# A gated-attention and MLP kernel: the table that gives small elementwise instructions to VectorE or GpSimd, and the written order, worked out anew

## The chip, the core and the metric

One Trainium2 chip, one of its cores. The metric is the device time of one execution in microseconds, median of three runs. The engines are called as in the profile: PE (TensorE), DVE (VectorE), ACT (ScalarE), POOL (GpSimd) and SP (SyncE, which issues all DMAs here). Each engine takes its own instructions in the order in which they are written, and waits at one whose inputs are not ready, while those behind it wait too.

## The reference

Two parts follow each other. The first is an attention with a complex, data-dependent decay, computed there as a recurrence over 768 steps (B, H, S, D = 4, 8, 768, 48):

```
mag = sqrt(a_re^2 + a_im^2);  a = a * min(mag, 0.999) / (mag + 1e-6)
for t in range(S):
    S_re, S_im = a_t * (S_re + i S_im)        # complex, row by row
    S_re = S_re + outer(k_t, v_t)
    y_t  = q_t @ S_re
```

The second treats y as 3072 tokens of 384 numbers and runs a small MLP over them: `h = y @ w_in` (384 to 2048), `g = h * clip(h + 3, 0, 6) / 6`, `out = g @ w_out` (2048 to 384).

## The kernel before

The 3072 tokens are cut into 24 chunks of 128 steps, and inside a chunk the recurrence becomes matrix products. Thirteen streams of work, each a Python generator, make the instructions:

- **normal** (letters N and O) brings the decays to their allowed size: squares, a logarithm and exponentials on ACT, and products on DVE or POOL (lines 399 to 424; tile `sq`).
- **chain** (C) multiplies the decays up along the 64 steps of each half of a chunk, three chunks at a time, in short DVE instructions (lines 439 to 483; tiles `pr`, `fx`, `z`), and then makes the small factors `t` and `ww` that carry the state from chunk to chunk (lines 489 to 523).
- **prep** (P, Q) makes the scaled keys and queries of a chunk (lines 553 to 569; tiles `gg`, `u`), which a DMA turns into `kq`.
- **mat** (A) runs a chunk's attention: `pA` on PE, masked on DVE into `am` (line 612), the running state (lines 631, 638, 679), and the result `py`, copied by ACT into `xh` (line 698) with its rounding rest `xl` on DVE (line 700).
- **moe** (M) runs the MLP over groups of chunks: seven groups of 2, 2, 4, 4, 4, 4 and 4 chunks. Each has 16 steps: `ph` on PE (line 750), `r` on ACT (line 757), then a product on DVE: `hs` in groups 0 and 1 (line 771), and `ph`, `gh`, `gl` on DVE, ACT, DVE from group 2 on (lines 761, 764, 767), where the products go to PE split into a high and a low half (lines 728 to 730).
- **weights** (W, D), **part** (I) and **wsplit** (S) turn the 16 blocks of weights into the form that PE uses (lines 340 to 358, 794 and 799, 814 and 817), and **verdict** (V) draws one flag `oki` from all range checks (lines 826 to 845); a fallback outside of this text would run if it were 0.

Nothing is scheduled by a tool at the places that matter here: under `manual_schedule` the string ORDER (lines 36 to 64, 2574 letters) says which stream makes its next step, and that is the order of the instructions on every engine:

```python
for x in ORDER:
    assert next(streams[x]) != "wait"
```

Which of the two engines takes one of some 200 small elementwise instructions is read from a second table, ENG (lines 66 to 80), one letter for each place and V for DVE:

```python
s = ENG.get(kind, "")
return V if i < len(s) and s[i] == "V" else P
```

The thirteen kinds stand for lines 402 (a), 412 (b), 555 (c), 561 (d), 799 (i), 523 (n), 817 (o), 489 (p), 631 (s), and 501 to 511 (t, u, v, w). Those of a to d, i, o and s work on 256 to 1024 columns and, all of them, read two inputs from SBUF; the other kinds work on 3 to 18 columns. The buffers matter in one place: `r`, `ot` and the verdict's `one` share a pool of two (tag `r`).

Of the kernel before, what the change touches and what calls it, by code (L numbers as in the profile page):

```python
# [35 lines left out]
ORDER = (
    "ZZNONOODWOWNOONWINWWZNOZOWNODNONOOWDNNDWQNNNWONINOWNOOWOZNNWONOOCWWCWCCCIZCWCCCCDDWCCNWCCCCWCWCN"
    "WCCWCCWCOCWCCCNCWINOCDCICCCNCNCWCWWWCDCCCCCCCCWCOWIWICOPCCOCCIWWWWCWPQPQPPWQPNWWQOWWOPPCPCNQPNDW"
    "WIWOWQPPPIPPDPWWQOCPAWWNPOQPQWCAWQWQWPWADCCPCACWQPAAWCAAPIAWWZWAWCICCCWWAPCIACCCCWCCWZAAWNWCACWA"
    "AAACPNCCACCCCCCPWADCAWAWWNWWAAACACADCNOCNOMMCMNCMMMWPWCACAWCCICAACAMWNCWMCAMMMCWCMWCMMONMWOMCWMC"  # L40
    "WACAMMMMCMMCWMCNMCMNIWMPMMMOWPMMWADCMCOPWPPMAWPOMMMODPCPCMOMMMWMAPMOWWMIICPCPAMIPPMIICCMMCCMIMCC"
    "APCCMPMCMPMPCMMMMMWPAAMMAMCCAMMPWMAAAMACDCIPWCMWCAPWAMMCAIPMPAMMCAMMWMWAMPWPPCMWPCWMCCWMCPCCAMCI"
    "CCCAWCWAWWCPMWMMCMPICMICMMMAMMAMCMCCCMAAMPMMMMMPCPCAMPCCMPZWCMAMMMMMCWMACWCPMSMAMMMZCAAPSAMMCMSC"
    "AMMMMAPPNMMMNSCASAINPMMPMMSMCMPCSPMOMAMIPNPMASPNNOAAMPMMMOPMPMPPMMAAOMNSONSMAAAAMAAMMMMCOAMOAMAA"
    "MPSCIMANOMOSMMMPSPAONPMMPMAMMPACPCPCMMAMSCPMMAMMMMPPPPMCSPMCACCAMAMMSMCIPACMAAAMMCCSMMMMPMMCAPIC"
    "CPCAMASACMCMMPMMCCPMMMCAMAMCCCMCACSPMAMSAASCCMMMIMAPAMMPMCCMMACZMMCMAACMMMZMCSCACSAAMPAMANMCMCCC"
    "AMCCNCCPAAMMMPMMCMCCMAOCANMNNMMAAACCCMMSCMMSMAMMSMPAAPMMMAOMPMPMAMNPMPNMPPMNMMMMPSCMMOOMPOSMMAOM"
    "NAMMPMMAOCMMCMAAMPMOMCMSNPMOMMPOMPMPCMCPAMMCCMPMPACPMMMCMMAACAMCMCMACACCPMMMMAMCPCMMCMCPPMMMMMCP"
    "CCCCCMMMAMAPPMCCMMMPMMCMMMCAPMAMMSCCMCCAMCMPMMMAPPMCMMAAPCPMCCCMMCCMCCMCMMMACMSPPMACMZAMMMCMNMCM"
    "ACMCCCCMPMANPPMCCPAMAMMNMAMMMMNAPAPAMPPMMMMAMMAMAMZNNAMPPAMMPOMPOAPMMNCPMOAPOMMOMMANMPPOAAAMACPM"  # L50
    "PMMCNMPAMPPSMCMMMOOMAMPAAOMMAMMMNMPMMMAMMPOPMPCPPMCMPACCMMPMMAAMCMPCCCAMCAPCAMCMMCPCMMMAMMACMMCM"
    "AAPCCCMACMCACMMCPPCPMMAAPMZMMAMAMCAMCMMCMMMZMMACCACMMCPCCMCMMNAMCCCNAAOMCMMNMMAACOCCMACNCCPMCMNA"
    "MPMNMCMNMMCMAAMCCMAMMMOMMMCAMAMCCMACONOMMAMMMMOMPAMPPMCAMMAAAMCOPPMCPAMMMPMMPPOMPMOMPMMNMMMMPAMP"
    "MMMMAOCAAMMPMPNPMMACCMCCAMCPMMCMMMMMPCAMMCCCCCMMPCPPMPAMMMAMAMMCMMCPMCCMMAMAMPPPPMCAMMAMMAAMMCCC"
    "APMPMMMCMACAMPPAMCACCMCMMAPACMAAPAMAMAMMCPCCMAMMMMMPCCMCCCPZCAMACMAMAACMMMZMMCCACCMNCMMNCCMMMCMN"
    "NMAPMCMMMOCMMMMCNAMPMMMMAAACOMNPOCAOOOMMACMMAMMCMPAPMMPMAMPMMMAPOMPPPCPMMMMPMPMMAMPOMMNMMMPPMCNM"
    "OMNAMONCMCPMPMAMAMCAMMMMCPMMMAMCMMAPMMMAPMAMCMMCMPMMCCMMCAMCMMCAAMPMMPMAMMMPMAPPMMCMAMCAMCCPCCPC"
    "AMCCMMAACAAAMMPMCMMCPCMCMAMMMAPCMMMMACMPCMACAPCAMAPAPCMMCCCCMCMPAMCMMMAMMMMMPCMAMAMMACMCMMAPACCM"
    "PAAMCAMMACMAMAMMPPAMCCCMMACMMAMMMACMMAMCMMMMAMACMMPMMPMMAMAPAMAAAPPPMPPCAMMMMMPMPAMMPMAAMCMMMMMM"
    "MMMMMMMMMAAMMMMMPMMMPMMMMAMMAACPPMMMAMAMPMMMMPMPMMMMPAPMMPMACAMMAMMPPMMMMMMAMPMPMMMPAPMPMMMPMMMA"  # L60
    "MMMPAMPPMMAMPMMMMMMAMMAMAMMMPAMMMAMAMPAAMMAPAMMMMAPPMMMMVMMMMMMMAMMMAMMMMAMMAAMAMMMAMAAMMMAMMMMM"
    "MAMMMAMAMMMMMMMMMMMMMMMMMMMMMMMMMMMMMMMMMMMMMMMMMMMMMMMMMMMMMMMMMMMMMMMMMMMMMMMMMMMMMMMMMMMMMMMM"
    "MMMMMMMMMMMMMMMMMMMMMMMMMMMMMMMMMMMMMMMMMMMMMMMMMMMMMMMMMMMMMMMMVMMMMMMMMMMMMM"
)
# [921 lines left out]
```

## Time and profile before

| | |
|---|---|
| median of 3 runs | 686.49 us (686.03 to 686.93) |
| the profiled execution | 686.5 us, its span 684.1 us |
| busy over the span: PE, DVE, ACT, POOL | 575.1, 557.1, 337.0, 138.2 us |
| instructions: PE, DVE, ACT, POOL | 4145, 1091, 636, 138 |
| PE's first matmul | at 71.3 us |
| DVE's first product (line 771) of group 1, and (line 761) of group 2 | ends at 170.8 and 250.8 us |
| ACT's first copy of a group's result (line 780), groups 2 to 6 | at 334.6, 428.1, 518.1, 604.8 and 675.1 us |

The 2.4 us between the span and the time lie around the program. In the rows below, a busy time is a union, while a mean is of single records, which overlap a little on DVE: an instruction's record starts some 0.08 us before that of the one ahead of it ends. A row of the views by line names the line, the engine, the operation, what it writes and reads, the shapes and the count; behind the bar stand the busy time in us and the mean in ns; behind the second bar the idle time just before.

### The profile page before, as it was taken

What the parts mean: (1) busy time and instruction counts of PE and PEld (TensorE: products, weight loads), DVE (VectorE), ACT (ScalarE), POOL (GpSimd) and SP (SyncE); (2) the same over time, 40 slices, a digit from 0 to 9 for tenths busy, and PEclk for the clock granted to TensorE, in tenths of its full rate; (3) what the DMA queues carried; (4) which work ended last, traced back from release to release, by engine and by line L of the source; (5) the groups of instructions that cost most, each with busy time, mean ns of one, the idle gap of its engine ahead of it and who ended that gap; (6) DMA issues with size and microseconds to landing.
All of it is one profiled execution on the core that took longest, in us unless ns stands there. A gap on an engine that the chain in (4) does not pass through costs nothing. (4 is left out here: it accounts for less than half of the span.)

```text
span 684.1 us, 11374 instructions
## 1 busy us (share of the span) xinstructions
PE 575.1 (84%) x4145; PEld 472.2 (69%) x4145; DVE 557.1 (81%) x1091; ACT 337.0 (49%) x636; POOL 138.2 (20%) x138
## 2 busy tenths in 40 slices
...
GB/s 337 117 115 84 235 173 161 36 130 110 148 98 97 121 86 76 75 91 121 135 94 163 3 97 97 167 51 97 86 51 105 97 26 74 62 47 0 1 0 52
DMA packets 51008, 66.97 MB, mean 98 GB/s; under 512 B 11905, under 2 KB 38401, under 8 KB 50945
## 3 DMA queue, kind: packets, MB, share of 16 engines
...
q8 instruction: 35, 0.57, 0.4%
...
## 5 line engine op out<-in xcount | busy, mean ns | idle before, releaser
L757 ACT ACTIVATE r<-ph,half 128x512 f32<-128x512 f32 (+1 forms) x112 | 70.0, 625 | 153.7 <-PE ph L750 153.3
L610 PE MATMUL pA<-kq 96*128 96x128 f32 x384 | 53.0, 288 | 71.9 <-DMA kq<-gg 71.3
L728 PE MATMUL po<-gl,wout_h 128*128 128x512 f32 x240 | 100.4, 418 | 6.4 <-DVE gl L767 6.4
L610 PEld LDWEIGHTS pA<-kq 96*128 96x128 f32 x384 | 51.7, 203 | 74.8 <-DMA kq<-gg 71.3
L761 DVE SCALAR_TENSOR_TENSOR ph<-r,ph 128x512 f32<-128x512 f32 x80 | 55.4, 692 | 58.4 <-ACT r L757 57.7
L729 PE MATMUL po<-gh,wout_l 128*128 128x512 f32 x240 | 95.2, 397 | 0.0
L730 PE MATMUL po<-gh,wout_h 128*128 128x512 f32 x240 | 94.9, 396 | 0.0
L764 ACT ACTIVATE gh<-ph 128x512 fp32r<-128x512 f32 x80 | 47.9, 598 | 84.0 <-DVE ph L761 83.9
L750 PE MATMUL ph<-xh,win_l 128*128 128x512 f32 (+1 forms) x288 | 81.6, 392 | 0.0
L750 PE MATMUL ph<-xh,win_h 128*128 128x512 f32 (+1 forms) x288 | 78.0, 379 | 0.0
L750 PE MATMUL ph<-xl,win_h 128*128 128x512 f32 (+1 forms) x288 | 77.3, 377 | 0.2 <-DVE xl L700 0.2
L767 DVE TENSOR_TENSOR gl<-ph,gh 128x512 fp32r<-128x512 f32 x80 | 55.0, 688 | 26.0 <-ACT gh L764 25.7
L439 DVE TENSOR_TENSOR pr<-z 128x288 f32<-128x288 f32 (+2 forms) x176 | 70.9, 433 | 1.4
L732 PE MATMUL po<-hs,wout 128*128 128x256 f32 x192 | 53.7, 409 | 13.2 <-DVE hs L771 13.1
L750 PEld LDWEIGHTS ph<-xh,win_l 128*128 128x128 f32 x288 | 52.7, 193 | 11.3 <-issue 0.6
L750 PEld LDWEIGHTS ph<-xl,win_h 128*128 128x128 f32 x288 | 51.7, 190 | 10.7 <-DVE xl L700 0.7
L728 PEld LDWEIGHTS po<-gl,wout_h 128*128 128x128 f32 x240 | 45.2, 188 | 19.9 <-DVE gl L767 8.9
L750 PEld LDWEIGHTS ph<-xh,win_h 128*128 128x128 f32 x288 | 51.6, 189 | 10.2 <-issue 0.8
L569 DVE TENSOR_TENSOR gg<-u,z 128x384 f32<-128x384 f32 x92 | 52.7, 618 | 0.3
L730 PEld LDWEIGHTS po<-gh,wout_h 128*128 128x128 f32 x240 | 45.1, 188 | 10.8
L729 PEld LDWEIGHTS po<-gh,wout_l 128*128 128x128 f32 x240 | 45.2, 188 | 8.2
L732 PEld LDWEIGHTS po<-hs,wout 128*128 128x128 f32 x192 | 34.9, 198 | 21.6 <-DVE hs L771 17.1
...
## 6 DMA issues: line engine op xcount, KB each, us to landing
kq<-gg SPq DMA_DIRECT2D x138, 128.0 KB, 4.6
...
```

The costliest lines, as they stand in the source:

```text
L439: V.tensor_tensor(pr[:, j], src, fac[:, j : j + 1].to_broadcast([C, *shape]), ALU.mult)
L569: V.tensor_tensor(gg[:, k, :, 1 - i].rearrange("p d (f s) -> p f d s", f=2), u[:, 2 * i : 2 * i + 2], zv[:, k], ALU.mult,)
L610: T.matmul(pA[:, i], kt[:, hf * 4 + i], qt[:, hf * 4 + i], start=True, stop=True)
L728: T.matmul(po[i], wh, gl, start=f == 0, stop=False)
L729: T.matmul(po[i], WOUTL[f][:, cols], gh, start=False, stop=False)
L730: T.matmul(po[i], wh, gh, start=False, stop=f == NFF - 1)
L732: T.matmul(po[i], WOUT[f][:, cols], hs[0], start=f == 0, stop=f == NFF - 1)
L750: T.matmul(ph, w[:, kt * C : (kt + 1) * C], xx[:, kt], start=t == 0 and kt == 0, stop=last)
L757: A.activation(r, ph, AF.Relu, scale=1.0 / 6.0, bias=half)
L761: V.scalar_tensor_tensor(ph, r, 1.0, ph, ALU.min, ALU.mult)
L764: A.activation(gh, ph, AF.Copy)
L767: V.tensor_tensor(gl, ph, gh, ALU.subtract)
```

## The change

Both tables are new, and nothing else is. ENG gives 126 of its 204 places to DVE where it gave 75: by kind, POOL keeps 3 (was 8) of a, 4 (11) of b, 11 (14) of c, 10 (17) of d, 5 (10) of i, 2 (7) of n, 6 (10) of o, 5 (5) of p, 11 (14) of s, and 21 (33) of t to w. ORDER has the same 2574 letters, each as often as before, in another sequence.

```diff
@@ ORDER, 2 of 27 lines @@
-    "ZZNONOODWOWNOONWINWWZNOZOWNODNONOOWDNNDWQNNNWONINOWNOOWOZNNWONOOCWWCWCCCIZCWCCCCDDWCCNWCCCCWCWCN"
-    "WCCWCCWCOCWCCCNCWINOCDCICCCNCNCWCWWWCDCCCCCCCCWCOWIWICOPCCOCCIWWWWCWPQPQPPWQPNWWQOWWOPPCPCNQPNDW"
...
-    "MMMMMMMMMMMMMMMMMMMMMMMMMMMMMMMMMMMMMMMMMMMMMMMMMMMMMMMMMMMMMMMMVMMMMMMMMMMMMM"
+    "ZZNODONZOWONWOOWDDNNNWWOOZDNWONWONZWONNNWOOOIDNOWONNWONZIONNOWONWNWPCCCCDWCCWCCNWCWCCWCNWCWCCCCC"
+    "CCCCWWCOCWWCNCOCCNCWWCWCOCDCCCCCCDWCNCNCCOWOCCWIWCCCQCIWCCWWCWCWPCOQCOOPWPICQWNPQPWIPQNWWQPQPWPP"
...
+    "MMMMMMMMMMMMMMMMMMMMMMMMMMMMMMMMMMMMMMMMMMMMMMMMMMMMMMMMMMMMMMMMMMMMMVMMMMVMMM"
@@ ENG @@
-    a="PVVPVVPVPVVPPVVVPP",
-    b="VVVPVVPPPPPPVPPPPV",
-    c="VPVPVPVVPPPPVPPVPPVVPPPV",
-    d="PPPVPPVPPPVVPPVVPPPPPPVP",
-    i="VPVPPVVPPPPVPVPP",
-    n="PPPPPPPV",
-    o="PPVVVPPPPPVPPPVV",
-    p="VPPPVPPV",
-    s="PPVPVPPVVPPPPPPVPVVVPVPV",
-    t="PPPVVVPPPPVPPPVP",
-    u="VPPPPPPPPPVPPVPV",
-    v="PPPPVVPV",
-    w="PPPVVVPP",
+    a="PVPVVVVVVVVVVVPVVV",
+    b="PVVVVVVVVVVPPVVPVV",
+    c="VVPVVVPVVPVPPPPPVVPVVPVP",
+    d="VVVPVVVPVVPVPVPPVPPPPVVV",
+    i="PVVPVVVVVPPVVVVP",
+    n="VPVVPVVV",
+    o="VPVVPPVVVVVVVPPP",
+    p="VPVPPPPV",
+    s="PPVVVVVVPVPVPPVVVPPPPVVP",
+    t="VVPVPPVPVPVVPVVV",
+    u="VVVVPPPPPVPVVVPV",
+    v="VPPPPVVV",
+    w="VPPPVVVP",
```

Three places show what that does to the engines' rows. The first is the beginning of POOL's own list, from its first instruction on tensors (`sq` of normal) to the time before PE starts. Before:

```order
L402 TENSOR_TENSOR sq<-sq 128x320
L402 TENSOR_TENSOR sq<-sq 128x256
L412 TENSOR_TENSOR sq<-sq,y_177 128x256
L799 TENSOR_TENSOR win_l<-win,win_h 128x384 x2
L555 TENSOR_TENSOR gge<-gge,ue 128x384
L561 TENSOR_TENSOR gg<-gg,u 128x384
L497 MEMSET ww 128x36
L501 TENSOR_TENSOR t<-pps,z 128x6 x2
L561 TENSOR_TENSOR gge<-gge,ue 128x384
L799 TENSOR_TENSOR win_l<-win,win_h 128x384
```

and now:

```order
L402 TENSOR_TENSOR sq<-sq 128x320
L412 TENSOR_TENSOR sq<-sq,y_133 128x320
L402 TENSOR_TENSOR sq<-sq 128x320
L799 TENSOR_TENSOR win_l<-win,win_h 128x384
L497 MEMSET ww 128x36
L555 TENSOR_TENSOR gg<-gg,u 128x384
L799 TENSOR_TENSOR win_l<-win,win_h 128x384
L489 COPY pps<-z 128x6x3
L561 TENSOR_TENSOR gg<-gg,u 128x384
```

The prep of the early chunk (`gge`) has left POOL, and so has one of the three `win_l` shown; one more step on `sq` of 320 columns has come.

The second place is DVE ahead of the first product of group 1 (`hs`, line 771, the last row of each). Before:

```order
L565 SCALAR_TENSOR_TENSOR u<-gg 128x2x192
L439 TENSOR_TENSOR pr<-z 128x144
L569 TENSOR_TENSOR gg<-u,z 128x2x3x64 x2
L441 TENSOR_TENSOR z<-pr 128x18x4
L443 TENSOR_TENSOR z<-pr 128x18x4
L569 TENSOR_TENSOR gg<-u,z 128x2x3x64 x2
L478 TENSOR_TENSOR fx<-z 128x441
L479 TENSOR_TENSOR z<-z 128x9x7x7
L612 TENSOR_TENSOR am<-pA,cst 128x512
L771 SCALAR_TENSOR_TENSOR hs<-r,ph 128x256
```

and now:

```order
L402 TENSOR_TENSOR sq<-sq 128x576
L478 TENSOR_TENSOR fx<-z 128x441
L479 TENSOR_TENSOR z<-z 128x9x7x7
L478 TENSOR_TENSOR fx<-z 128x441
L479 TENSOR_TENSOR z<-z 128x9x7x7
L481 TENSOR_TENSOR z<-z,fx 128x9x7x7
L483 TENSOR_TENSOR z<-z,fx 128x9x7x7
L412 TENSOR_TENSOR sq<-sq,y_1311 128x576
L478 TENSOR_TENSOR fx<-z 128x441
L479 TENSOR_TENSOR z<-z 128x9x7x7
L799 TENSOR_TENSOR win_l<-win,win_h 128x384
L771 SCALAR_TENSOR_TENSOR hs<-r,ph 128x256
```

Instead of a chunk's prep (lines 565 and 569) and a mask (line 612), the step of the chain (lines 478 to 483) stands there, among it instructions that POOL had: `sq` (lines 402, 412) and `win_l` (line 799).

The third place is the end of SP's list, where the last results are written out and the flag is read. Before:

```order
L584 DMA kq<-gg 16x8x256 x6
L592 DMA vt<-in_vL_dram 128x512
L781 DMA out_dram<-ot 128x512 x3
L879 TENSOR_LOAD oki
L879 ISA x2
L781 DMA out_dram<-ot 128x512 x3
L883 COMPARE_AND_BRANCH
```

and now:

```order
L584 DMA kq<-gg 16x8x256 x6
L592 DMA vt<-in_vL_dram 128x512
L781 DMA out_dram<-ot 128x512 x5
L879 TENSOR_LOAD oki
L879 ISA x2
L781 DMA out_dram<-ot 128x512
L883 COMPARE_AND_BRANCH
```

The flag's load stood ahead of the last three writes, and now stands ahead of the last one alone. On DVE and PE the flag's instructions (lines 836 to 845, 842) have moved to behind the last product and the last matmul of group 6.

## Rows read from the trace of the kernel before

**Rows 1.** The view of windows: busy time of each engine in four stretches. Columns: stretch and its length, busy us (and instructions) of PE, PEld, DVE, ACT and POOL, granted clock of PE as a share, share of the DMA engines, GB/s. The stretches end with PE's first matmul, with DVE's first product of group 1, with its first of group 2, and with the middle of the run behind that.

```profile
0.00:71.30 71.30, 0.01 (x1) 0.04 (x1) 58.01 (x121) 53.31 (x102) 15.22 (x25) 1.00 0.52 164
71.30:170.80 99.50, 84.21 (x578) 69.91 (x578) 97.84 (x208) 63.71 (x123) 28.88 (x22) 0.98 0.57 140
170.80:250.80 80.00, 71.77 (x660) 62.57 (x660) 76.49 (x142) 38.53 (x84) 31.90 (x26) 0.94 0.57 118
250.80:520.00 269.20, 264.32 (x1969) 215.53 (x1970) 251.57 (x501) 127.65 (x238) 53.72 (x55) 1.00 0.45 93
```

**Rows 2.** The timeline of DVE and POOL from 26 to 34 us: start, length, engine, line, operation, what it writes and reads, shapes, count.

```profile
26.51 1.63 DVE L439 TENSOR_TENSOR pr<-z 128x288 f32<-128x288 f32 x2
26.55 1.28 POOL L799 TENSOR_TENSOR win_l<-win,win_h 128x384 fp32r<-128x384 f32 x1 [4.28 <-ACT win_h L794]
...
31.14 0.55 DVE L346 SCALAR_TENSOR_TENSOR wout<-ws 128x384 int32<-128x384 int32 x1
31.61 0.82 DVE L439 TENSOR_TENSOR pr<-z 128x288 f32<-128x288 f32 x2
...
33.77 0.75 DVE L402 TENSOR_TENSOR sq<-sq 128x576 f32<-128x576 f32 x1
```

**Rows 3.** The same view at 212 us.

```profile
212.26 2.01 POOL L631 TENSOR_TENSOR state<-state,cw 96x1024 f32<-96x1024 f32 x1
...
212.40 2.99 DVE L443 TENSOR_TENSOR z<-pr 128x144 f32<-128x144 f32 x1
```

**Rows 4.** Groups by line and shape on DVE from the start to 250.8 us.

```profile
L439 DVE TENSOR_TENSOR pr<-z 128x288 f32<-128x288 f32 x56 | 26.2, 504 | 0.4
L569 DVE TENSOR_TENSOR gg<-u,z 128x384 f32<-128x384 f32 x32 | 20.2, 677 | 0.0
L342 DVE SCALAR_TENSOR_TENSOR ws<-ws 128x768 int32<-128x768 int32 x16 | 16.8, 1052 | 3.4 <-ACT ws L340 3.4
...
L479 DVE TENSOR_TENSOR z<-z 128x441 f32<-128x441 f32 x16 | 12.5, 780 | 0.6
L612 DVE TENSOR_TENSOR am<-pA,cst 128x512 f32<-128x512 f32 x17 | 11.4, 680 | 0.6 <-PE pA L610 0.6
L443 DVE TENSOR_TENSOR z<-pr 128x144 f32<-128x144 f32 x28 | 11.1, 396 | 0.0
...
L346 DVE SCALAR_TENSOR_TENSOR wout<-ws 128x384 int32<-128x384 int32 x16 | 10.8, 676 | 0.0
...
L481 DVE TENSOR_TENSOR z<-z,fx 128x441 f32<-128x441 f32 x8 | 6.5, 810 | 0.0
...
L817 DVE TENSOR_TENSOR wout_l<-wout,wout_h 128x384 fp32r<-128x384 f32 x4 | 3.9, 985 | 0.0
...
L424 DVE SCALAR_TENSOR_TENSOR z<-z,sq 128x320 f32<-128x320 f32 x1 | 1.0, 1030 | 0.0
```

**Rows 5.** The same view from 98 to 117 us, a stretch in which POOL does next to nothing.

```profile
L479 DVE TENSOR_TENSOR z<-z 128x441 f32<-128x441 f32 x4 | 2.5, 619 | 0.1
...
L481 DVE TENSOR_TENSOR z<-z,fx 128x441 f32<-128x441 f32 x2 | 1.2, 610 | 0.0
...
L346 DVE SCALAR_TENSOR_TENSOR wout<-ws 128x384 int32<-128x384 int32 x2 | 1.1, 550 | 0.0
L342 DVE SCALAR_TENSOR_TENSOR ws<-ws 128x768 int32<-128x768 int32 x1 | 1.0, 959 | 0.2 <-ACT ws L340 0.2
...
L799 DVE TENSOR_TENSOR win_l<-win,win_h 128x384 fp32r<-128x384 f32 x1 | 0.6, 551 | 0.0
```

**Rows 6.** The same view from 33.1 to 44.3 us, in which POOL does nothing.

```profile
L439 DVE TENSOR_TENSOR pr<-z 128x288 f32<-128x288 f32 x6 | 2.5, 452 | 0.1
...
L443 DVE TENSOR_TENSOR z<-pr 128x144 f32<-128x144 f32 x3 | 0.9, 299 | 0.0
```

**Rows 7.** Groups by line and shape on POOL from the start to 250.8 us.

```profile
L799 POOL TENSOR_TENSOR win_l<-win,win_h 128x384 fp32r<-128x384 f32 x10 | 12.2, 1220 | 26.8 <-ACT win_h L794 22.3 <-issue 4.6
L817 POOL TENSOR_TENSOR wout_l<-wout,wout_h 128x384 fp32r<-128x384 f32 x9 | 11.1, 1237 | 36.4 <-issue 18.1 <-ACT wout_h L814 12.1 <-ACT kk L623 6.3
L561 POOL TENSOR_TENSOR gg<-gg,u 128x384 f32<-128x384 f32 x6 | 10.1, 1680 | 15.2 <-DMA vt<-in_vL_dram 8.0 <-ACT u L559 7.2
L412 POOL TENSOR_TENSOR sq<-sq,y 128x576 f32<-128x576 f32 x4 | 6.7, 1678 | 13.4 <-ACT y L408 13.4
L631 POOL TENSOR_TENSOR state<-state,cw 96x1024 f32<-96x1024 f32 x3 | 6.6, 2204 | 0.0
L555 POOL TENSOR_TENSOR gg<-gg,u 128x384 f32<-128x384 f32 x3 | 5.5, 1850 | 28.4 <-ACT u L553 28.4
L402 POOL TENSOR_TENSOR sq<-sq 128x576 f32<-128x576 f32 x3 | 5.4, 1811 | 16.3 <-ACT sq L399 16.3
```

**Rows 8.** The view of waits from 170.8 to 250.8 us: who waited for whom, us in total, times, longest.

```profile
PE po L732 <- DVE hs L771: 5.8, 3, 2.8
```

**Rows 9.** The timeline of ACT and of SP's queue at the end.

```profile
675.05 1.30 ACT L780 ACTIVATE ot<-po 128x512 f32<-128x512 f32 x2 [1.85 <-PE po L730]
...
675.68 3.50 SPq L781 DMA_DIRECT2D out_dram<-ot  x3
...
678.22 0.60 ACT L780 ACTIVATE ot<-po 128x512 f32<-128x512 f32 x1 [1.87 <-PEq L883]
```

**Rows 10.** From the page, what the DMA engines moved in GB/s, in 40 equal slices of the span.

```profile
GB/s 337 117 115 84 235 173 161 36 130 110 148 98 97 121 86 76 75 91 121 135 94 163 3 97 97 167 51 97 86 51 105 97 26 74 62 47 0 1 0 52
```

More of the change, by code (lines that the diff above doesn't have):

```diff
@@ L36 @@
 ORDER = (
-    "ZZNONOODWOWNOONWINWWZNOZOWNODNONOOWDNNDWQNNNWONINOWNOOWOZNNWONOOCWWCWCCCIZCWCCCCDDWCCNWCCCCWCWCN"
-    "WCCWCCWCOCWCCCNCWINOCDCICCCNCNCWCWWWCDCCCCCCCCWCOWIWICOPCCOCCIWWWWCWPQPQPPWQPNWWQOWWOPPCPCNQPNDW"
-    "WIWOWQPPPIPPDPWWQOCPAWWNPOQPQWCAWQWQWPWADCCPCACWQPAAWCAAPIAWWZWAWCICCCWWAPCIACCCCWCCWZAAWNWCACWA"
-    "AAACPNCCACCCCCCPWADCAWAWWNWWAAACACADCNOCNOMMCMNCMMMWPWCACAWCCICAACAMWNCWMCAMMMCWCMWCMMONMWOMCWMC"
-    "WACAMMMMCMMCWMCNMCMNIWMPMMMOWPMMWADCMCOPWPPMAWPOMMMODPCPCMOMMMWMAPMOWWMIICPCPAMIPPMIICCMMCCMIMCC"
@@ L42 @@
[L42 to L61, printed above, removed]
@@ L62 @@
-    "MAMMMAMAMMMMMMMMMMMMMMMMMMMMMMMMMMMMMMMMMMMMMMMMMMMMMMMMMMMMMMMMMMMMMMMMMMMMMMMMMMMMMMMMMMMMMMMM"
-    "MMMMMMMMMMMMMMMMMMMMMMMMMMMMMMMMMMMMMMMMMMMMMMMMMMMMMMMMMMMMMMMMVMMMMMMMMMMMMM"
+    "ZZNODONZOWONWOOWDDNNNWWOOZDNWONWONZWONNNWOOOIDNOWONNWONZIONNOWONWNWPCCCCDWCCWCCNWCWCCWCNWCWCCCCC"
+    "CCCCWWCOCWWCNCOCCNCWWCWCOCDCCCCCCDWCNCNCCOWOCCWIWCCCQCIWCCWWCWCWPCOQCOOPWPICQWNPQPWIPQNWWQPQPWPP"
+    "NWNOQPOCCPCPWAIWWWPQCCWQCQPCACAWACDQWAACCWCPIAAPWCPWCPAAACPDWWACWPCAWPCICWWAWCWACQACZCAAACCAACWC"
```

23 lines of the change are left out of this document (added).

## The prediction

> **What bounds the kernel now.** I read the windows first, because the page's shares are means over stages with different limits. Until 71.3 us PE has nothing to do. From there to 250.8 us, where DVE makes the first product of group 2, DVE is busy 174.3 of 179.5 us and PE 156.0 [rows 1]: DVE sets the pace. PE's idle time there is mostly a wait for DVE; near group 1, 5.8 us of it hang on `hs` [rows 8]. From 250.8 to 520 us the roles turn: PE is busy 264.3 of 269.2 us and DVE 251.6 [rows 1]; behind that PE goes on without a gap. So the end is about PE's time from group 2 on, which the change does not alter (the order puts the same matmuls behind that point), plus the moment at which group 2 starts. That moment is DVE's, and the question is what the new tables do to DVE's work up to it.
>
> The second view is DVE's groups by line. Not all of DVE's busy time is work. At 26.5 us two L439 take 1.63 us while a `win_l` runs on POOL for 1.28 us [rows 2]; a pair of them takes 0.82 us a few microseconds later, with POOL idle [rows 2]. At 212.4 us an L443 that takes 0.30 us elsewhere [rows 6] lasts 2.99 us beside a POOL instruction of 1024 columns and 2.01 us [rows 3]. DVE instructions with two inputs in SBUF are held, those that read PSUM are not: L612 keeps its 680 ns beside all of POOL's work [rows 4].
>
> **What the held time amounts to, before 250.8 us.** Count times (mean here less mean where POOL is still) [rows 4 to 6]: L439 56 x (504 - 452) = 2.9 us; L569 32 x (677 - 550, the L346 of the same 384 columns) = 4.1; L479 16 x (780 - 619) = 2.6; L443 28 x (396 - 299) = 2.7; L346 into `wout` 16 x (676 - 550) = 2.0; L481 8 x (810 - 610) = 1.6; L817 4 x (985 - 551) = 1.7. That is 17.6 us. Eleven other forms, from L342 with 16 x (1052 - 959) = 1.5 down to the single L424 with about 0.5 [rows 4, 5], add 12.2. Together 29.8 us, an eighth of DVE's 232.3 busy us there. Up to that point POOL has run 43 instructions of 256 to 1024 columns, the 38 of [rows 7] and five single ones; they have 19,456 columns. So one POOL column costs DVE 1.53 ns: 0.59 us for 384 columns, 0.88 for 576, 1.57 for 1024.
>
> **What the same instruction costs on DVE.** From the start of one 384-column instruction to that of the next it is 31.61 - 31.14 = 0.47 us [rows 2]: its record of 0.55 overlaps the next by 0.08. The same 0.08 off gives 0.67 us for 576 columns (0.75 in [rows 2]) and, by the slope between these two, 1.14 us for 1024. Per column it is cheaper to do the work on DVE than to be held by POOL.
>
> **The change, up to group 2.** By the order DVE gets 13 more instructions of 384 columns (13 x 0.47 = 6.1 us), 8 of 576 (5.4), 3 of 1024 (3.4), 8 small ones of some 0.1 us (0.7), one L414 more and a closing pair of chain products less (-0.4): +15.2 us. POOL keeps 15 of the 43, with 5,824 columns. They will hold DVE for 5,824 x 1.53 = 8.9 us instead of 29.8: 20.9 come back. The three of 1024 columns all leave POOL ahead of that point, and the one that [rows 3] shows cost DVE 2.99 - 0.30 = 2.69 us, where its columns give 1.57. If all three cost that, the others' rate is (29.8 - 8.1) / 16,384 = 1.33 ns and the 15 keep 7.7 us: 22.1 come back. The sum is so 15.2 - 20.9 = -5.7 or 15.2 - 22.1 = -6.9 us; I take -6.5. It lies wholly on the path as long as DVE sets it. The bounds: if each of the 15 held DVE for its own whole length (0.9 to 1.9 us, 20 together, by the means of [rows 7]) it would be +5.7; if none held it, -14.6. I stay with the rate, since the 15 are of the same lines and stand among the same DVE work as the 43.
>
> Moved waits come beside it. DVE's idle time is 13.3 us before PE's start, 5.2 us from there to 250.8 [rows 1], so waits that go can give little after the start; new ones could cost. I take 0, between -5 and +5. The loads: the fourth piece of the first decays goes behind two more blocks of weights of 768 KB on SP; at the 337 GB/s of the first slice [rows 10] that is 4.7 us later at most. ACT has a block of weights to convert ahead of that piece in the new order: 0, at most +4.7. ACT and PE do what they did, in another sequence.
>
> **From group 2 to group 5.** The order adds 4.5 us to DVE here and takes 3,072 POOL columns away, 4.7 us at the rate above: 0, or +4.5 if nothing came back. DVE has 17.6 us to spare in this stretch, PE 4.9 [rows 1], so a part of it is covered. I take +0.5.
>
> **The end.** The flag's nine DVE instructions and its matmul now stand behind the last product. DVE is done with them about 2 us later, when PE has just finished; the second `ot` shares a buffer with the verdict's `one`. The last `ot` starts at 678.22 us in any case, since its buffer waits for the write issued at 675.68 [rows 9], and the flag's load on SP, ahead of the last write, should be through by then. +0.1; +1 if not.
>
> Sum: 686.5 (the profiled execution; the median is 686.49) - 6.5 + 0.5 + 0.1 = 680.6 us, with its own range of 675 to 685.
>
> **A rule that speaks against it.** DVE is the engine that has nothing to spare before 250.8 us [rows 1], and the change gives it more. The Trainium skill, Perfetto Trace Analysis, section "Optimizing Scalar/DVE Operations", says that with DVE saturated it may make sense to offload work, even to GpSimd; it adds that between these two it might not help, because they share a read port. By its first half the move back costs the 15.2 us and the time would be some 702 us; by its second half, which [rows 2, 3] bear out, the held time comes back.
>
> **Rivals.**
>
> 1. *Group 1 does not get shorter (slower).* The gain isn't spread evenly. Up to group 1's first product the order puts 15.5 us more on DVE and takes 6,784 POOL columns (10.4 us) away: that product comes 5.1 us later, at 175.9 us, as more of the chain and of the weights now stands ahead of it. The forecast needs the stretch from there to group 2 to shrink from 80.0 to 68.4 us. If it takes as long as before, group 2 starts 5.1 us late: 686.5 + 5.1 + 0.6 = 692.2 us. It decides from 74.3 us on. For it: PE is busy 71.8 of the 80 us [rows 1], and its list is fixed. Against it: DVE is busy 76.5 there, POOL 31.9 [rows 1], so the held time is largest there, and PE's idle time is a wait for DVE [rows 8].
> 2. *PE sets that stretch.* If PE needs its 71.8 busy us [rows 1] and no less, group 2 starts at 247.7: -3.1, and the time is 686.5 - 3.1 + 0.6 = 684.0 us.
> 3. *The held time does not come back (slower).* The 15 that stay would have to hold DVE 2.0 us each for that, 29.8 in all as before; then the 15.2 us come on top: 686.5 + 15.2 = 701.7 us. Against it: those lines last 1.2 to 1.9 us as a mean (all but L631, which is gone there) [rows 7].
> 4. *More than forecast.* The waits that shrink, too: a third of the 13.3 us before PE's start and PE's 4.9 us later [rows 1], -9: 671 to 675.
> 5. *Nothing to be seen.* New waits on DVE of about 6 us eat the gain: 685 to 688.
>
> **How the numbers follow.** Forecast 0.53; rivals 1 to 5: 0.17, 0.11, 0.03, 0.10, 0.06. A measurement of this kernel can tell about 0.2% from no change, that is 685.1 to 687.9. Faster: 0.53 + 0.10 + half of rival 2 (0.06) = 0.69. Within 0.2%: the other half and rival 5 = 0.11. Slower: rivals 1 and 3 = 0.20. The predicted time is the forecast's. The range reaches down to 671 for rival 4 and up to 690, which takes in rivals 2 and 5 and the nearer half of rival 1; I leave out its farther half, rival 3 and a little below, some 0.15.
>
> **What would show it.** In the new profile POOL's instructions should fall to some 85 and its busy time to about 80 us, DVE's busy time should stay within 10 us of 557 although it has 51 more instructions, and the means of L439, L569 and L443 up to group 2 should drop to within 30 ns of 452, 550 and 299. Group 1's first product should come near 176 us, group 2's first near 244, and each later group's results 5 to 8 us earlier than 334.6, 428.1, 518.1, 604.8 and 675.1. PE's first matmul should come about a microsecond before 71.3. The prediction is wrong in its main step if those means stay up, in its second if the stretch of group 1 stays near 80 us with DVE idle, and in its third if the gain at group 2 is there and is lost later.

## The result, and the profile after

| | before | after |
|---|---|---|
| median of the runs | 686.26 us (684.15 to 686.93, 4 runs) | 665.98 us (664.57 to 669.69, 4 runs) |
| the profiled execution, its span | 686.5, 684.1 us | 666.9, 665.0 us |
| DVE's first product of group 1 ends | 170.8 | 168.1 (forecast 175.9) |
| DVE's first product of group 2 ends | 250.8 | 233.1 (forecast near 244) |
| from there to the first product of group 5 | 273.1 us | 272.2 us (forecast +0.5) |
| from there to the end | 160.2 us | 159.7 us |

The ratio is 0.9718, with an interval of 0.9671 to 0.9764: faster, and by 20 us where the prediction said 6. It lies below the range of 671 to 690. A second set of five runs of the changed kernel, beside later experiments, gave 666.22 us and a ratio of 0.9692 (0.967 to 0.9715); its profile put the two first products at 168.1 and 232.8 us. Three later runs whose DVE has the same work up to there, those that leave out something behind group 2, put them at 167.9 to 169.4 and at 231.7 to 234.0, so a moment that differs by less than some 2 us says little; the stretch from group 2 to group 5 is 272.2 us in both profiles of the changed kernel.

Nearly all of the gain, 17.7 of 19.1 us of span, is there when group 2 starts. The view of windows of the changed kernel, over the same stretches as [rows 1] (stretch, its length, busy us of PE, PEld, DVE, ACT, POOL, granted clock, DMA share, GB/s):

```profile
0.00:71.30 71.30, 1.86 (x9) 1.89 (x10) 59.73 (x139) 51.09 (x99) 4.66 (x15) 1.00 0.51 157
71.30:170.80 99.50, 85.17 (x677) 72.78 (x676) 97.83 (x227) 72.23 (x140) 7.85 (x10) 0.91 0.70 170
170.80:250.80 80.00, 76.36 (x687) 66.66 (x686) 76.53 (x166) 42.42 (x91) 15.59 (x21) 0.98 0.46 92
250.80:520.00 269.20, 267.30 (x1931) 219.14 (x1930) 243.50 (x509) 124.06 (x232) 37.40 (x36) 0.99 0.45 96
```

DVE is as busy in the first three stretches as it was, and makes 532 instructions there instead of 471. PE's wait for `hs` ahead of group 2 is down from the 5.8 us of [rows 8]; in the view of waits from 168 to 233.1 us, and with the view of windows from group 1's to group 2's first product:

```profile
PE po L732 <- DVE hs L771: 2.1, 2, 1.7
...
168.10:233.10 65.00, 62.70 (x571) 56.41 (x572) 61.97 (x140) 35.00 (x76) 10.97 (x14) 0.97 0.53 106
```

The groups on DVE up to group 2's first product, by line and shape, answer to [rows 4]:

```profile
L439 DVE TENSOR_TENSOR pr<-z 128x288 f32<-128x288 f32 x56 | 24.1, 458 | 0.2
L569 DVE TENSOR_TENSOR gg<-u,z 128x384 f32<-128x384 f32 x32 | 16.0, 549 | 0.0
L342 DVE SCALAR_TENSOR_TENSOR ws<-ws 128x768 int32<-128x768 int32 x16 | 15.2, 951 | 3.4 <-ACT ws L340 3.4
...
L612 DVE TENSOR_TENSOR am<-pA,cst 128x512 f32<-128x512 f32 x16 | 10.9, 681 | 0.7 <-PE pA L610 0.7
L479 DVE TENSOR_TENSOR z<-z 128x441 f32<-128x441 f32 x16 | 9.9, 619 | 0.6
...
L346 DVE SCALAR_TENSOR_TENSOR wout<-ws 128x384 int32<-128x384 int32 x16 | 8.8, 549 | 0.0
...
L443 DVE TENSOR_TENSOR z<-pr 128x144 f32<-128x144 f32 x28 | 8.4, 299 | 0.0
```

Each mean is, to a few ns, that of [rows 5, 6], where POOL does nothing. POOL does something here, 16 instructions of 256 columns or more; DVE hardly notices them. (The forecast said 15 with 5,824 columns. The trace has 16 with 6,144: POOL's list shown ahead of the prediction has three of 320 columns now, where it had one, and not one more as the text there says.) That is more than was forecast, and two places show why. In the timeline of the changed kernel (start, length, engine, line, operation, tiles):

```profile
196.90 0.55 DVE L817 TENSOR_TENSOR wout_l<-wout,wout_h 128x384 fp32r<-128x384 f32 x1
197.37 0.68 DVE L612 TENSOR_TENSOR am<-pA,cst 128x512 f32<-128x512 f32 x1
...
197.80 1.01 POOL L817 TENSOR_TENSOR wout_l<-wout,wout_h 128x384 fp32r<-128x384 f32 x1 [9.12 <-ACT wout_h L814]
...
197.97 0.41 DVE L771 SCALAR_TENSOR_TENSOR hs<-r,ph 128x256 f32<-128x256 f32 x1
...
198.30 0.68 DVE L612 TENSOR_TENSOR am<-pA,cst 128x512 f32<-128x512 f32 x1
...
224.58 0.55 DVE L817 TENSOR_TENSOR wout_l<-wout,wout_h 128x384 fp32r<-128x384 f32 x1
...
224.74 1.66 POOL L412 TENSOR_TENSOR sq<-sq,y 128x576 f32<-128x576 f32 x1 [12.73 <-ACT y L408]
...
225.05 0.41 DVE L771 SCALAR_TENSOR_TENSOR hs<-r,ph 128x256 f32<-128x256 f32 x1
...
225.38 0.68 DVE L679 TENSOR_TENSOR state<-pG,state 96x512 f32<-96x512 f32 x1
...
225.98 0.54 DVE L700 TENSOR_TENSOR xl<-py,xh 128x384 fp32r<-128x384 f32 x1
```

The `wout_l` on POOL at 197.80 us runs beside L612, L771 and L612 on DVE, the `sq` at 224.74 beside L771, L679 and L700. All of these read one operand from PSUM (`pA`, `ph`, `pG`, `py`), and each takes as long as without POOL (L612's mean is 681 ns above, 680 in [rows 4]). The `wout_l` on DVE at 224.58 us reads two operands from SBUF; it had begun when the `sq` started, and keeps its 0.55 us, while that `sq` lasts 1.66 us and the one at 295.56 below 1.43. Behind group 2 this is not so everywhere. At 295 us an L402 that takes 0.75 us alone [rows 2] lasts 3.11 us, with three instructions of POOL beside it; the L761 ahead of it, which reads PSUM, keeps its 0.69:

```profile
293.65 1.94 POOL L631 TENSOR_TENSOR state<-state,cw 96x1024 f32<-96x1024 f32 x1
...
294.86 0.69 DVE L761 SCALAR_TENSOR_TENSOR ph<-r,ph 128x512 f32<-128x512 f32 x1 [0.71 <-ACT r L757]
295.47 3.11 DVE L402 TENSOR_TENSOR sq<-sq 128x576 f32<-128x576 f32 x1
295.56 1.43 POOL L412 TENSOR_TENSOR sq<-sq,y 128x576 f32<-128x576 f32 x1
...
296.96 1.00 POOL L817 TENSOR_TENSOR wout_l<-wout,wout_h 128x384 fp32r<-128x384 f32 x1
...
297.93 1.51 POOL L561 TENSOR_TENSOR gg<-gg,u 128x384 f32<-128x384 f32 x1
```

To have one measure for all kernels, I split DVE's time from the start of one instruction to the start of the next into four: the idle time before the next; the time that this form takes with POOL still (its work); what is left over while a POOL instruction runs (held); what is left over else. Up to group 2's first product, in us (DVE's first instruction starts at 6):

| | work | idle | held | else | first product of group 2 |
|---|---|---|---|---|---|
| before | 195.7 | 12.5 | 31.7 | 5.5 | 250.8 |
| after | 210.7 | 10.3 | 2.6 | 4.1 | 233.1 |

So: +15.0 of work, -29.1 of held time, -2.2 of idle time, -1.4 else, -17.7 in all.

### The profile page after: what moved, and what is told of

Read it like the earlier page. It is cut to its first block, busy times and chain, and to the rows that moved or that the text cites. A ratio compares the mean times of both kernels' runs of the same rounds, so it can differ in the third digit from the quotient of the medians.

```text
span 665.0 us, 11344 instructions
## 1 busy us (share of the span) xinstructions
PE 566.6 (85%) x4145; PEld 470.0 (71%) x4145; DVE 537.2 (81%) x1142; ACT 335.3 (50%) x636; POOL 69.2 (10%) x87
## 4 chain that ended last, share of the span: by engine, by line
PE 54%; DVE 26%; issue 8%; DMA 6%; ACT 3%; SPq 2%; POOL 1%; DVEq 0%; POOLq 0%; ACTq 0%
PE ph L750 21%; PE po L728 8%; PE po L729 7%; PE po L730 7%; PE pA L610 4%; PE py L651 4%; DVE pr L439 3%; DVE gg L569 3%; DMA kq<-gg 3%; PE pG L675 2%; DVE ws L342 2%; DVE z L441 1%; DVE z L479 1%; DVE ph L761 1%; DVE gl L767 1%
## 5 line engine op out<-in xcount | busy, mean ns | idle before, releaser
L610 PE MATMUL pA<-kq 96*128 96x128 f32 x384 | 53.4, 287 | 72.7 <-DMA kq<-gg 69.4
L761 DVE SCALAR_TENSOR_TENSOR ph<-r,ph 128x512 f32<-128x512 f32 x80 | 55.4, 693 | 70.0 <-ACT r L757 69.7
L764 ACT ACTIVATE gh<-ph 128x512 fp32r<-128x512 f32 x80 | 47.8, 597 | 78.4 <-DVE ph L761 78.4
L439 DVE TENSOR_TENSOR pr<-z 128x288 f32<-128x288 f32 (+2 forms) x176 | 63.9, 392 | 1.2
L732 PE MATMUL po<-hs,wout 128*128 128x256 f32 x192 | 50.3, 393 | 7.6 <-DVE hs L771 7.6
L569 DVE TENSOR_TENSOR gg<-u,z 128x384 f32<-128x384 f32 x92 | 46.0, 551 | 0.2
```

The lines of the kernel that those rows point to most:

```text
L439: V.tensor_tensor(pr[:, j], src, fac[:, j : j + 1].to_broadcast([C, *shape]), ALU.mult)
L569: V.tensor_tensor(gg[:, k, :, 1 - i].rearrange("p d (f s) -> p f d s", f=2), u[:, 2 * i : 2 * i + 2], zv[:, k], ALU.mult,)
L610: T.matmul(pA[:, i], kt[:, hf * 4 + i], qt[:, hf * 4 + i], start=True, stop=True)
L732: T.matmul(po[i], WOUT[f][:, cols], hs[0], start=f == 0, stop=f == NFF - 1)
L761: V.scalar_tensor_tensor(ph, r, 1.0, ph, ALU.min, ALU.mult)
L764: A.activation(gh, ph, AF.Copy)
```

## The experiments

Two theories stood against each other. Mine, from the rows above: what a POOL instruction costs DVE depends on what DVE does beside it, and the new order has put POOL's beside DVE instructions that read PSUM, so table and order belong together. The rival: the number of POOL's columns decides, as the prediction had it, and the table alone brings the gain, or the order alone does. The first products of groups 1 and 2, the stretch from there to group 5's first product, and the end of the span, in us, from each kernel's profile:

| kernel | group 1 | group 2 | to group 5 | end | median, ratio to before (interval) |
|---|---|---|---|---|---|
| before | 170.8 | 250.8 | 273.1 | 684.1 | 686.26 |
| after | 168.1 | 233.1 | 272.2 | 665.0 | 665.98, 0.9718 (0.9671 to 0.9764) |
| old order, new table | 167.9 | 242.4 | 283.5 | 686.4 | 687.56, 1.0009 (0.9993 to 1.0025) |
| new order, old table | 177.6 | 253.5 | 280.6 | 694.0 | 696.39, 1.0152 (1.0124 to 1.0179) |
| as many on POOL, other places | 173.1 | 242.4 | 272.5 | 674.4 | 680.32, 0.9925 (0.9899 to 0.995) |
| all on DVE | 173.2 | 243.1 | 279.5 | 683.2 | 683.81, 0.9946 (0.9922 to 0.997) |
| less DVE up to group 2 | 164.2 | 225.0 | 271.3 | 657.1 | 662.04, 0.9663 (0.961 to 0.9715) |
| less DVE behind group 2 | 168.1 | 233.1 | 269.5 | 663.1 | 664.76, 0.969 (0.9657 to 0.9723) |
| less PE behind group 2 | 167.9 | 231.7 | 269.1 | 660.4 | 662.75, 0.9659 (0.9618 to 0.9699) |
| less of both behind group 2 | 169.4 | 234.0 | 266.6 | 660.7 | 661.31, 0.9602 (0.9556 to 0.9647) |
| more on POOL | 168.3 | 231.7 | 270.7 | 661.8 | 664.15, 0.9684 (0.9657 to 0.9711) |

**The old order with the new table.** The kernel before with ENG alone replaced (its first two lines here):

```diff
 ENG = dict(
-    a="PVVPVVPVPVVPPVVVPP",
-    b="VVVPVVPPPPPPVPPPPV",
+    a="PVPVVVVVVVVVVVPVVV",
+    b="PVVVVVVVVVVPPVVPVV",
...
```

> The old order with the new table: the 51 instructions move from POOL to DVE, and nothing else changes. My theory: the changed kernel gains because the time for which POOL's instructions hold DVE's has gone from some 32 to some 2.5 us before group 2; fewer instructions on POOL give some two thirds of that, and the new order gives the rest, by putting those that stay beside DVE instructions that read PSUM. Here only the first works: up to group 2 DVE has 16.0 us more work than before, 14 POOL instructions with 5,248 columns are left and hold it at the old rate of 1.53 ns a column, 8 us. Group 2's first product near 243 us, the time 677 to 681 us. Rival 1 (the table alone does it, wherever the instructions stand): 664 to 668 us. Rival 2 (the order alone does it, through better filled waits): no gain, 684 to 700 us.

It came out as no change, 687.56 us. Up to group 2 it does about what the prediction said of the whole change: -8.4 us, with 7.1 us held by 15 POOL instructions. Behind that it loses 10.4 us again: DVE has 4.9 us more work there, held time fell only from 18.5 to 16.9, where the changed kernel with the same table has 9.4, and DVE is idle for 26.2 us instead of 19.2, with longer waits for `r` of ACT (11.3 us, 5.4 before) and for `state` of POOL (3.4, none before). The old order was not made for this table; which of its places costs the waits was not tried. Its view of waits behind group 2 (who for whom, us, times, longest; PE's wait for `gl` is 4.8 us in the kernel before and 1.4 us in the changed one):

```profile
PE po L728 <- DVE gl L767: 7.0, 8, 2.0
...
DVE ph L761 <- ACT r L757: 11.3, 10, 2.2
...
DVE state L638 <- POOL state L631: 3.4, 2, 2.2
```

**The new order with the old table.** The changed kernel with ENG of before:

```diff
 ENG = dict(
-    a="PVPVVVVVVVVVVVPVVV",
-    b="PVVVVVVVVVVPPVVPVV",
+    a="PVVPVVPVPVVPPVVVPP",
+    b="VVVPVVPPPPPPVPPPPV",
...
```

> The new order with the old table: 51 instructions go back to POOL. Up to group 2 DVE has 194.2 us of work (before: 195.1; changed: 210.2) and 42 POOL instructions with 19,456 columns beside it, which the new order was not made for. My theory: they hold DVE at about the old rate, 25 to 32 us, and waits for POOL's slower instructions come on top: group 2's first product between 243 and 255 us, the time 676 to 690 us. Rival 2 (the order alone does it): the held time stays small, group 2 starts near 218 us, and the time is 650 to 664 us.

Longer, 696.39 us: 33.1 us held up to group 2, where the kernel before has 31.7, and 15.5 us idle (12.5 before). Neither half brings anything alone, and the times expected of both were too short: 677 to 681 us with the table alone, 676 to 690 with the order alone.

**As many on POOL, at other places.** The changed kernel with the P's of the six large kinds but `s` moved to a neighbouring place each, so that POOL gets as many instructions, but other ones:

```diff
-    a="PVPVVVVVVVVVVVPVVV",
-    b="PVVVVVVVVVVPPVVPVV",
-    c="VVPVVVPVVPVPPPPPVVPVVPVP",
-    d="VVVPVVVPVVPVPVPPVPPPPVVV",
-    i="PVVPVVVVVPPVVVVP",
+    a="VPVPVVVVVVVVVVVPVV",
+    b="VPVVVVVVVVPVVPVVPV",
+    c="VVVPVVVPVVPPPPVVPPVPVVPP",
+    d="VVVVPVVVPVVPVPVPPPPVVPPV",
+    i="VPVVPVVVPVVPVVPV",
...
-    o="VPVVPPVVVVVVVPPP",
+    o="VVPPVVPVVVVVPVPP",
```

> The changed kernel with the same number of instructions on POOL, but others of the same kinds: of the kinds on lines 402, 412, 555, 561, 799 and 817 each that POOL had goes to DVE and a neighbour in the table goes to POOL. Up to group 2 DVE has 210.4 us of work (changed: 210.2) and 17 POOL instructions of 256 columns or more with 6,976 columns (changed: 15 with 5,824). My theory: these stand beside any DVE instruction, hold it at the old rate of 1.53 ns a column, 10.7 instead of some 2.5 us, and the time is 671 to 677 us. Rival 3 (only the number on POOL matters): 665 to 668 us.

680.32 us: 14 of the 20 us are gone, more than expected (671 to 677). The profile is of the shortest of its five runs, 676.31 us; its span is 9.4 us longer than the changed kernel's, and 9.3 of that is there at group 2. What makes the other four runs some 4 us longer still is open. DVE's work up to group 2 is the same as in the changed kernel (210.9 us), its held time is 11.7 instead of 2.6. POOL has one instruction and 832 columns more up to there (table below), which at the prediction's rate cost 1.3 us. Its timeline at 225.9 us shows a `wout_l` beside the chain's products, which read both operands from SBUF:

```profile
225.90 2.12 POOL L817 TENSOR_TENSOR wout_l<-wout,wout_h 128x384 fp32r<-128x384 f32 x1 [12.66 <-ACT wout_h L814]
...
227.03 1.04 DVE L441 TENSOR_TENSOR z<-pr 128x36 f32<-128x36 f32 x1
...
228.48 1.41 POOL L412 TENSOR_TENSOR sq<-sq,y 128x576 f32<-128x576 f32 x1 [0.46 <-ACT y L408]
...
228.62 1.32 DVE L441 TENSOR_TENSOR z<-pr 128x36 f32<-128x36 f32 x1
```

A `wout_l` takes 1.01 us at 197.80 in the changed kernel and this one 2.12, and an L441 of 36 columns takes more than a microsecond twice. This is the run that decides between the theories. Held time up to group 2 by POOL column:

| kernel | POOL instructions of 256 columns or more, their columns | held, us | ns a column | how many of them run beside a DVE instruction that reads PSUM |
|---|---|---|---|---|
| before | 43, 19,456 | 31.7 | 1.63 | 14 |
| new order, old table | 42, 19,456 | 33.1 | 1.70 | 9 |
| old order, new table | 15, 5,568 | 7.1 | 1.28 | 4 |
| as many, other places | 17, 6,976 | 11.7 | 1.68 | 3 |
| after | 16, 6,144 | 2.6 | 0.42 | 12 |

Four kernels agree with the prediction's 1.53 to some 0.25 ns. Only the one whose order and table were made together falls out, and the last column says why. Counted in time, these POOL instructions run beside DVE work that reads PSUM for 10.0 of their 17.8 us in the changed kernel, and for 8 to 13% of their time in the other four. For each us beside DVE work with both operands in SBUF the five are of one size: 0.48 to 0.71 us held, 0.49 in the changed kernel (2.6 us in 5.3).

**All on DVE.** The changed kernel with every letter of ENG a V (one line of thirteen):

```diff
-    a="PVPVVVVVVVVVVVPVVV",
+    a="VVVVVVVVVVVVVVVVVV",
...
```

> The changed kernel with all 204 places on DVE, so that POOL has only its few memsets. Up to group 2 DVE has 218.7 us of work (changed: 210.2) and nothing holds it: +8.5 - 2.5 = +6 us at group 2. From there to group 5 it has 249.6 instead of 232.1 us of work, 17.5 more, against 9.4 us held and 22 us idle: 0 to +8. My theory: 672 to 680 us, and every mean on DVE at its unheld value. If POOL's instructions were still the trouble in the changed kernel, it would be faster than that one, below 664 us.

683.81 us, 4 to 12 more than I expected. Nothing is held, but DVE's work up to group 2 is 219.3 us, 8.6 more than after, and 249.6 instead of 232.1 from there to group 5. So POOL is worth 18 us to the changed kernel: it takes 26 us of work from DVE and takes 12 back in held time (2.6 and 9.4); the rest is waits.

**What POOL holds, form by form.** One form behind the other, each with 24 DVE instructions (ND) and, but for the first, twelve POOL instructions (NP) of 128x384; `x` and `j` lie in SBUF, `pin` in PSUM:

```diff
+    def pool_two(k):
+        for _ in range(NP):
+            P.tensor_tensor(p[k], x, j, ALU.mult)
...
+    def dve_two(k):
+        for _ in range(ND):
+            V.tensor_tensor(d[k], x, j, ALU.mult)
+
+    def dve_psum(k):
+        for _ in range(ND):
+            V.tensor_tensor(d[k], pin, j, ALU.mult)
...
```

> This kernel leaves the whole computation out and only sets VectorE and GpSimd side by side: 24 VectorE instructions of one form (128x384), alone, and then beside twelve GpSimd instructions of 128x384, form after form. If GpSimd holds only those VectorE instructions that read both operands from SBUF: tensor_tensor (0.47 us alone) and scalar_tensor_tensor from two SBUF tiles last about 1.2 to 1.6 us on the mean while GpSimd runs, the same tensor_tensor with one operand in PSUM stays within 0.05 us of its time alone, and so do tensor_scalar and copy, which read one operand, though GpSimd may be held by them. The rival, that the number and size of GpSimd's instructions alone decide (the rate of 1.53 ns a column that the prediction went by): every form with two operands gets longer by the same, some 0.6 us for each GpSimd instruction, the PSUM form among them.

Its groups by line (L47 alone; L51 two tiles of SBUF; L55 one of PSUM and one of SBUF; L59 `scalar_tensor_tensor` on two of SBUF; L63 and L67 one operand; L71 as L51, but beside the POOL copies of L43):

```profile
L51 DVE TENSOR_TENSOR d<-x,j 128x384 f32<-128x384 f32 x24 | 21.5, 895 | 0.8
L59 DVE SCALAR_TENSOR_TENSOR d<-x,j 128x384 f32<-128x384 f32 x24 | 21.5, 895 | 0.8
L67 DVE COPY d<-j 128x384 f32<-128x384 f32 x24 | 16.8, 698 | 0.8
L63 DVE TENSOR_SCALAR d<-j 128x384 f32<-128x384 f32 x24 | 16.7, 698 | 0.8
L71 DVE TENSOR_TENSOR d<-x,j 128x384 f32<-128x384 f32 x24 | 15.6, 650 | 0.8
L47 DVE TENSOR_TENSOR d<-x,j 128x384 f32<-128x384 f32 x24 | 13.4, 559 | 0.8
L55 DVE TENSOR_TENSOR d<-pin,j 128x384 f32<-128x384 f32 x24 | 13.4, 557 | 0.8
```

With an operand in PSUM DVE takes 557 ns beside POOL and 559 alone. With two tiles of SBUF it loses 24 x (895 - 559) = 8.1 us to twelve POOL instructions, 0.67 us each or 1.75 ns a column, near the 1.53 of the prediction: that rate is the price of standing beside such work, not of a POOL instruction as such.

**DVE less loaded up to group 2, and behind it.** The same line in two runs, 16 instructions each time; first those of the first four chains, then (with `q < 4` in the edit) those of the last four:

```diff
-                V.tensor_tensor(zs[:, k], zs[:, k], fac[:, 0].to_broadcast(shape), ALU.mult)
+                if q > 3:
+                    V.tensor_tensor(zs[:, k], zs[:, k], fac[:, 0].to_broadcast(shape), ALU.mult)
```

> Leaves out a part of the computation: the 16 VectorE instructions of L479 that belong to the first four chains, 16 x 0.62 = 9.9 us, all up to group 2's first product in the changed kernel. If VectorE alone sets the pace there, the first product of group 2 comes 9 to 10 us earlier (at 223 to 224 instead of 233.1) and the time is 656 to 657. If GpSimd, ScalarE or TensorE is close behind by now, less comes through: 661 to 666.

> The counterpart: leaves out the 16 instructions of the same line that belong to the last four chains, again 9.9 us of VectorE, all between group 2's and group 5's first products. If TensorE alone sets the pace there (267 of 269 us busy), the stretch stays at 271 to 273 us and the time at 665 to 667. If VectorE's time still counts there (232 us of work, 9 us held, 8 us of small losses), some of it comes through: 656 to 662.

Up to group 2, 8.1 of the 9.9 us come through, and 7.9 are there at the end of the profiled span. The four timed runs fall into two pairs (658.7 and 658.9, 665.2 and 665.5), and the profile is of the faster one; the slower one lies within the range of the changed kernel's own runs, and what parts them is open. Behind group 2 only 2.7 of 9.9 come through. By the profiles, DVE sets the pace up to group 2 in the changed kernel, too, and hardly behind it.

**PE less loaded behind group 2.**

```diff
                 for kt in range(3):
                     last = kt == 2 and t == len(terms) - 1
-                    T.matmul(ph, w[:, kt * C : (kt + 1) * C], xx[:, kt], start=t == 0 and kt == 0, stop=last)
+                    if t == 0 and g in (2, 3, 4):
+                        continue
+                    first = kt == 0 and t == (1 if g in (2, 3, 4) else 0)
+                    T.matmul(ph, w[:, kt * C : (kt + 1) * C], xx[:, kt], start=first, stop=last)
```

> Leaves out a part of the computation: the three matmuls with win_l of every step of groups 2, 3 and 4, 144 matmuls, 42 us of TensorE by the rows of the changed kernel. If TensorE alone sets the pace there, the stretch from group 2's first product to group 5's falls by 36 to 42 us. If VectorE, whose work with what is held there is 250 us, is next behind it, the stretch falls only to about 250 us and the time by 19 to 23 us, to 643 to 647.

My 42 us counted whole records of matmuls that overlap. The view of windows, of the changed kernel and of this one over the stretch from group 2 to group 5, shows what PE's busy time lost, 20.8 us:

```profile
233.10:505.30 272.20, 268.86 (x1991) 220.01 (x1990) 249.65 (x522) 127.19 (x239) 39.10 (x41) 0.99 0.45 93
```

```profile
231.70:500.80 269.10, 248.10 (x1848) 197.93 (x1849) 249.22 (x522) 126.61 (x239) 39.21 (x41) 0.97 0.46 94
```

The stretch got 3.1 us shorter, not some 22. PE, with 248 of 269 us busy, now waits for DVE, whose busy time is the same 249 us; the waits of PE and of DVE in this run (lines are moved by three: L770 is `gl`, L764 `ph`, L760 `r`):

```profile
PE po L728 <- DVE gl L770: 17.0, 16, 2.6
...
DVE ph L764 <- ACT r L760: 6.5, 9, 1.6
DVE gl L770 <- ACT gh L767: 6.2, 12, 0.7
```

**Both at once.** The two edits behind group 2 together.

> Leaves out both at once: the 9.9 us of VectorE of the last four chains and the 42 us of TensorE of groups 2 to 4, each of which alone shortened the stretch from group 2's to group 5's first product by 3 us (272.1 to 269.5 and 269.1). If the two engines are limits side by side there, the stretch now falls by clearly more than the sum of the two, to 258 to 263 us. If a third thing (the chain of hand-overs between TensorE, ScalarE and VectorE in each step) bounds it, it stays at 266 to 269 us.

266.6 us, the third thing rather than two limits side by side: 5.6 us less than after, the sum of the two alone (2.7 and 3.1) and no more. PE is busy for 250.2 of the 266.6 us and DVE for 241.6, and they wait for each other by way of ACT. That the hand-overs of each step bound it, in the written order, fits these waits; it was not tried by itself. PE's granted clock, 0.96 of the upper level here and 0.99 in the changed kernel, may be a part of it.

**More on POOL.** The changed kernel with all small kinds on POOL, and with three of 384 columns that DVE did shortly ahead of instructions that read PSUM:

```diff
-    i="PVVPVVVVVPPVVVVP",
-    n="VPVVPVVV",
-    o="VPVVPPVVVVVVVPPP",
+    i="PVVPVVVVPPPVPVVP",
+    n="PPPPPPPP",
+    o="VPVVPPVVPVVVVPPP",
...
```

> The changed kernel with more given to GpSimd: every one of the small copies and products of a few columns (L489 to L523), and three instructions of 384 columns that stand on VectorE where its next instructions read PSUM (L799 at 136.3 and at 187.3, L817 at 234.7). By the theory that GpSimd holds VectorE only where both of VectorE's operands are in SBUF, up to group 2 it takes 1.1 us (two of the three) and about 13 x 0.17 = 2.2 us from VectorE and gives back less than 1 us of held time: group 2's first product 1 to 2.5 us earlier than the 233.1 of the changed kernel. By the rate of 1.53 ns a column the two large ones alone give back 1.2 us, and nothing or a loss of up to 1 us remains. A rival is the longer way of the small ones through GpSimd (0.2 us each, one after the other, ahead of six DMAs that a later step waits for): the later groups wait, and the time is 1 to 3 us longer.

Beside it on the same chip:

> The changed kernel once more, beside the two runs that follow: 664 to 669.

664.15 us (662.46 to 667.0) against 666.22 (663.5 to 666.75) of the changed kernel; the intervals of the ratios overlap, so this is not shown to be faster. The profile has group 2 1.4 us earlier than the first profile of the changed kernel and 1.1 earlier than the second, as expected, but no more than runs with the same DVE work there differ by; the end comes 2.8 us earlier than the second's. Held time up to group 2 did not stay within the expected 1 us: by the same split it is 1.9 us more than in the changed kernel. The three were picked for what stood behind them on DVE, at 136.3, 187.3 and 234.7 us; POOL came to them earlier, at 128.4, 180.0 and 225.0 us, and so beside other DVE work, as with the last (an L479 takes 0.62 us alone):

```profile
224.96 1.55 POOL L817 TENSOR_TENSOR wout_l<-wout,wout_h 128x384 fp32r<-128x384 f32 x1
...
225.68 1.31 DVE L479 TENSOR_TENSOR z<-z 128x441 f32<-128x441 f32 x1
```

## Why the prediction was wrong

By its own steps:

- **What bounds the kernel.** Right up to group 2: the run with less DVE there gives back 8.1 of 9.9 us. Behind group 2 "PE goes on without a gap" was read from busy time, and as a cause it does not hold: with 21 us of PE's busy time gone, 3 us came back.
- **The held time of the kernel before.** 29.8 us by means, 31.7 by the split. Right.
- **What the change adds to DVE.** +15.2 us forecast, +15.0 measured. Right.
- **The 15 that stay on POOL: the step that failed.** They were to hold DVE for 8.9 us, or 7.7 by the lower rate. They are 16, and hold it for 2.6. The reason given was that they "stand among the same DVE work as the 43". They do not: in the new order 12 of the 16 run beside an instruction that reads PSUM, where 14 of the 43 did. The prediction said itself that those are not held; the step used a mean over the old neighbours and did not ask for the new ones. With as many at other places of the new order the mean holds (1.68 ns a column), and with the new order and its own table it does not (0.42).
- **Moved waits.** 0, between -5 and +5; measured -2.2 of idle time and -1.4 of small losses, within the bounds. So the 12.0 us from the step's -5.7 (with 8.9 held) to the measured -17.7 are 6.3 of held time that the 15 did not cost, 1.9 of held time that the kernel before had beyond the 29.8, 3.6 of moved waits and small losses, and 0.2 of work.
- **The stretch from group 1 to group 2**, which had to shrink from 80.0 to 68.4 us, took 65.0. Rival 1 (80.0) and rival 2 (PE needs 71.8) fell with it: PE's wait for `hs` there, 5.8 us in [rows 8], is down to 2.1. PE's list for the stretch was not fixed, as rival 1 had it: the new order puts more matmuls ahead of group 1's product, and 571 instead of 660 stand in the stretch, for which PE is busy 62.7 of the 65.0 us. Group 1 itself came at 168.1 and not 5 us late, since 1.6 us is held ahead of it, where the rate gives 5.0 for POOL's 3,264 columns there, and since waits and small losses fell by some 3 us.
- **From group 2 to group 5 and the end.** +0.5 and +0.1 forecast, -0.9 and -0.5 measured. Right in size, though the same step failed here, too: held time fell by 9.1 us (18.5 to 9.4), not by 4.7, and hardly any of that shows. And +0.5 was a property of this order and not of the stretch, which is 8 to 10 us longer with table and order apart.
- **The rule that spoke against it.** Its first half would have cost 15 us, and the time fell by 20. With everything on DVE the changed kernel loses 18 us, so work on POOL pays where POOL's instructions stand beside DVE work that is not held; at other places it was worth 3 us (680.32 against 683.81). The Trainium skill, SBUF — State Buffer, section "Who interferes with whom", says that a DVE instruction with two SBUF inputs contends with a GpSimd instruction that reads SBUF, and one with at most one SBUF input, outside certain faster modes, does not; the 895 and 557 ns above agree.
- **What would show it.** POOL has 87 instructions (85 forecast) and 69.2 us busy (80): its instructions are shorter in the mean, `wout_l` 1.04 us where it took 1.25. DVE's busy time fell to 537.2 us, 20 and not at most 10 from 557. The means came to within 6 ns of the three named ones. The groups' results come at 318.3, 407.9, 499.6, 584.9 and 656.1 us, 16 to 20 earlier (5 to 8 forecast), and PE's first matmul at 69.4, 1.9 us earlier (1).

The rival "more than forecast" had the right direction, but by waits, which gave some 3 of its 9 us, and with 671 as its lower end.
